# Causal masks of the first tiles and the first six head pairs as a VectorE product, and the first sequence loaded by head pair with weight quarters between

## The chip, the cores and the metric

The kernel runs on one core of one Trainium2 chip. The metric is device time in microseconds (us) of one execution, the median of several. A profiled span (314.4 us for the kernel before) is a little shorter than the timed execution (315.6 us), so spans are compared with spans and times with times.

Engine names in the profile: PE is TensorE (matmuls), PEld is TensorE loading weights, DVE is VectorE, ACT is ScalarE, POOL is GpSimd, SP is SyncE.

## The reference

Two stages. Attention with chunk selection: each query takes the 6 chunks of 32 keys (out of 24) with the highest upper bound, under a causal mask. Then a feed-forward layer with a squared ReLU over all tokens.

```python
batch, n_heads, seq, head_dim = 4, 8, 768, 64          # attention
n_tokens, d_model, d_ff = 3072, 512, 2048              # feed-forward

ub = sum(max(q * k_min[chunk], q * k_max[chunk]))      # upper bound of each chunk
ub = where(query_chunk >= chunk, ub, -1e9)
top_chunks = argsort(ub)[-6:]
mask = selected(top_chunks) & (query >= key)
attn = softmax(where(mask, q @ k.T / 8, -1e9))
x = attn @ v                                           # heads side by side: (3072, 512)
out = relu(x @ w_in) ** 2 @ w_out
```

## The kernel before

Inputs are fp32 in HBM and bf16 on chip. Loads that convert are issued by GpSimd, one instruction for each load. A sequence has 768 tokens, that is 6 tiles of 128, and 8 heads, handled as 4 head pairs; 4 sequences make 16 pairs.

The first tile of every sequence needs no selection, because it has only four chunks; the kernel does these tiles first, and their feed-forward runs beside the attention of sequence 0. From then on the attention of one sequence runs beside the feed-forward of the one before it. The feed-forward of the last sequence runs alone at the end.

The loads: first tiles of k, q, v for two sequences at a time, then the other tiles of sequence 0 as one load for each tile of all heads, then weights, then the other sequences.

```python
def load_rest(nm, b, j):            # one tile of 128 tokens, all 8 heads: 128 KB as bf16
    ...
    nc.gpsimd.dma_start(
        out=nat[nm, b][:, j - 1, :, 0:D],
        in_=SRC[nm][b, :, 128 * j:128 * (j + 1)].rearrange("h p d -> p h d"))
# ... (first loads and constants cut)
for nm in "kq":
    for j in range(1, NT):
        load_rest(nm, 0, j)
load_w_in(4, 8)
```

The causal mask of a diagonal 128x128 block is a GpSimd instruction, in the same stream as the load issues. It stands between the exponential (ScalarE) and the product with v (TensorE):

```python
def causal(e, n):
    nc.gpsimd.affine_select(
        out=e, in_=e, compare_op=ALU.is_ge, fill=0.0, base=0,
        channel_multiplier=-1, pattern=[[0, n], [1, 128]])
# first tiles, for each sequence b and half hh of the pairs:
    nc.scalar.activation(e, ps, ACT.Exp, scale=scale)
    causal(e, NP)                                     # 128x512
# pairs, for each of five banks of scores, four of which hold diagonal blocks:
    nc.scalar.activation(e, ps, ACT.Exp, scale=scale)
    if diagonal:
        causal(e[:, 128*d0:128*d1]..., d1 - d0)       # 128x128 or 128x256
    run_ffn()                                         # some feed-forward units
    behind.append(lambda: values(...))                # product with v, three banks later
    if i % 2 == 0:
        beside()                                      # next piece of the next pair's selection
```

The selection of a pair (stage a) transposes k on TensorE, takes chunk maxima and minima on VectorE (`kr`, 0.95 us each), transposes q, forms its positive and negative parts (`qp`, `qm`), multiplies for the upper bounds (`ub`), takes the top 8 of each row and turns the selection into extra rows of q, from which the scores (`ps`) then follow. The order of instructions on each engine is fixed when the kernel is built, by a scheduler. In the traces below each engine takes its instructions in that order, so one that waits holds those behind it: in the run loads_only, eight masks that stand behind loads in GpSimd's stream begin only at 40.05 us, when the last of those loads has been issued.

The softmax here doesn't subtract the row's maximum and nothing guards it: scores larger than these inputs give would overflow.

## Time and profile before

| | before |
|---|---|
| time, median | 315.6 us |
| first scores of pair 0 | 35.91 us |
| first 320-column up-projection: end of the first sequence's stage | 98.5 us |
| the same for the next two sequences | 158.6, 217.2 us |
| span of the profile | 314.4 us |

The first-tile feed-forward uses 512-column matmuls, the later ones 320-column matmuls, so the first 320-column up-projection marks the moment when the first sequence is done and the next begins. The steady stage takes 58.6 us. Lines of TensorE's timeline, from three stretches (start us, duration us, what): the last q transpose of pair 0, its first scores, and the first 320-column up-projection.

```profile
28.34 0.29 PE L246 MATMUL qT<-ident,qn 128*128 128x128 bf16 x1 [0.55 <-DMA qn<-in_q_dram]
35.91 1.04 PE L398 MATMUL ps<-qsc,kqc 88*128 88x256 bf16 x4
98.53 0.71 PE L315 MATMUL ph<-xT,w_in_sb 128*128 128x320 bf16 x4
```

The page of the kernel before, part 2: busy tenths in 40 slices of 7.86 us, and the mean DMA share.

```profile
PE   0554887898888999999999999999999999899995
POOL 8966962999968011111120111212011122000000
DMA  9999999999999100010100000111000011100021
GB/s 68 174 168 125 134 189 196 155 131 137 171 148 109 11 1 2 2 67 35 68 3 3 0 2 33 41 62 36 2 0 2 2 68 36 67 0 2 14 89 67
```

GpSimd is at 9 in slices 8 to 11 (55 to 86 us), and TensorE doesn't reach 9 for good until slice 14 (102 us). The engines' busy times in stretches of the start and the first sequence, and of a steady stretch at the end (after the stretch and its length, one column each for PE, PEld, DVE, ACT and POOL: busy us and, in brackets, instructions; then granted clock, DMA share, GB/s):

```profile
24.00:36.00 12.00, 6.95 (x66) 4.74 (x67) 10.06 (x38) 2.34 (x4) 9.67 (x16) 1.00 1.20 109
46.00:56.00 10.00, 7.44 (x68) 4.00 (x66) 7.60 (x24) 6.88 (x13) 3.87 (x10) 1.00 1.55 194
56.00:66.00 10.00, 9.47 (x86) 5.84 (x89) 6.30 (x25) 7.57 (x14) 10.00 (x18) 0.83 2.41 154
66.00:76.00 10.00, 8.73 (x87) 5.26 (x87) 6.05 (x13) 6.39 (x12) 10.00 (x17) 1.00 1.92 123
160.00:200.00 40.00, 38.68 (x374) 25.47 (x374) 29.63 (x103) 30.73 (x64) 6.25 (x20) 1.00 0.04 14
```

From 56 to 76 us GpSimd never rests. The chain of waits of the kernel before in that stretch, in order of time (start us, duration us, what), shows what it does:

```profile
...
61.47 1.59 POOL e L168 x5
63.06 0.86 POOL vn L86
63.92 0.89 POOL kn L86
64.81 0.55 POOL e L168 x2
65.36 0.84 POOL kn L86
66.20 0.67 POOL e L168
66.87 2.61 POOL kn L86 x3
...
```

Masks (`e L168`) stand between load issues (`L86`) of the next sequences' tiles at about 0.9 us each. Who pays is in the list of waits of the weight loads between 36 and 99 us (total us, times, longest us):

```profile
PEld L381 <- POOL e L168: 7.9, 7, 3.1
```

The product with v takes a masked tile as its weights; it waits seven times, 7.9 us in all, and the matmuls of that product wait with it.

### The profile page before, as it was taken

How to read it: one execution, taken by the hardware profiler on the slowest of the kernel's cores; microseconds unless marked ns; L12 is line 12 of the kernel's file. 1: busy time of each engine (PE TensorE's matmuls, PEld its weight loads, DVE VectorE, ACT ScalarE, POOL GpSimd, SP SyncE). 2: the span in 40 equal slices, each digit the busy share in tenths (PEclk: the TensorE clock that was granted, in tenths of full speed). 3: DMA queues.
4: the chain of work that ended last, by engine and by line, in shares of the span. 5: the costliest groups of instructions: out<-in, count | busy, mean ns of one | idle time of the engine just before them, and what ended most of it. 6: DMA issues, size and time to landing. Idle time of an engine off the chain costs nothing.

```text
span 314.4 us, 6653 instructions
## 1 busy us (share of the span) xinstructions
PE 276.2 (88%) x2503; PEld 171.8 (55%) x2528; DVE 183.6 (58%) x595; ACT 189.4 (60%) x370; POOL 112.0 (36%) x222
## 2 busy tenths in 40 slices
PE   0554887898888999999999999999999999899995
PEld 0332644555446666655677665557676555566542
DVE  0117978485647888646598886657887640455200
ACT  2212267586466879666597886567789666377311
POOL 8966962999968011111120111212011122000000
PEclk9999999799999999999999999999999999999999
DMA  9999999999999100010100000111000011100021
GB/s 68 174 168 125 134 189 196 155 131 137 171 148 109 11 1 2 2 67 35 68 3 3 0 2 33 41 62 36 2 0 2 2 68 36 67 0 2 14 89 67
DMA packets 82188, 20.61 MB, mean 66 GB/s; under 512 B 75332, under 2 KB 78572, under 8 KB 82156
## 3 DMA queue, kind: packets, MB, share of 16 engines
q0 software_dynamic: 78448, 13.64, 55.2%
q1 hardware_dynamic: 3708, 6.55, 5.7%
q8 instruction: 20, 0.33, 0.4%
q14 instruction: 12, 0.10, 0.1%
HBM read 27.26 MB, written 6.29 MB: 107 GB/s over the span
## 4 chain that ended last, share of the span: by engine, by line
PE 48%; POOL 17%; DMA 11%; DVE 11%; ACT 8%; issue 3%; ACTq 0%; POOLq 0%
PE ph L315 18%; PE py L330 16%; DMA w_out_sb<-in_moe_w_out_dram 6%; POOL vn L86 5%; PE ps L398 5%; DVE kr L234 5%; ACT qsc L254 4%; PE av L381 4%; POOL qn L86 4%; DMA w_in_sb<-in_moe_w_in_dram 4%; POOL e L168 3%; DVE kqc L231 3%; POOL kn L86 3%; ACT ht L320 2%; DMA qn<-in_q_dram 2%
## 5 line engine op out<-in xcount | busy, mean ns | idle before, releaser
L405 ACT ACTIVATE e<-ps 128x512 bf16<-128x512 f32 x160 | 92.4, 601 | 51.9 <-PE ps L398 50.3
L315 PE MATMUL ph<-xT,w_in_sb 128*128 128x320 bf16 (+1 forms) x572 | 98.6, 307 | 1.2 <-issue 0.2
L168 POOL TENSOR_SCALAR_AFFINE_SELECT e<-e 128x128 bf16<-128x128 bf16 (+2 forms) x136 | 47.3, 356 | 143.1 <-ACT e L405 140.5
L330 PE MATMUL py<-w_out_sb,h 128*128 128x512 bf16 x363 | 94.0, 378 | 0.9
L320 ACT ACTIVATE ht<-ph 128x320 bf16<-128x320 f32 (+1 forms) x144 | 64.7, 457 | 25.2 <-PE ph L315 16.1
L315 PEld LDWEIGHTS <-w_in_sb 128*128 128x128 bf16 x576 | 55.3, 97 | 29.1 <-issue 7.3
L398 PE MATMUL ps<-qsc,kqc 88*128 88x128 bf16 (+1 forms) x320 | 61.8, 278 | 0.5
L323 DVE TENSOR_TENSOR h<-ht 128x320 bf16<-128x320 bf16 (+1 forms) x144 | 47.2, 339 | 22.7 <-ACT ht L320 21.6
L381 PEld LDWEIGHTS <-e 128*128 128x128 bf16 x640 | 38.3, 98 | 30.8 <-POOL e L168 9.6
L330 PEld LDWEIGHTS <-h 128*128 128x128 bf16 x384 | 36.5, 97 | 29.0 <-issue 0.2
L381 PE MATMUL av<-vn,e 128*128 128x65 bf16 x480 | 38.6, 194 | 6.7 <-POOL e L168 6.3
L234 DVE TENSOR_REDUCE kr<-kT 128x24 bf16<-128x768 bf16 x32 | 29.2, 951 | 0.2
L231 DVE COPY kqc<-kT 64x768 bf16<-64x768 bf16 x32 | 17.7, 553 | 15.9 <-PE kT L227 15.4
L335 ACT COPY ob<-py 128x512 f32<-128x512 f32 x24 | 14.0, 585 | 21.1 <-PE py L330 21.0
L398 PEld LDWEIGHTS <-kqc 88*128 88x128 bf16 x320 | 23.1, 100 | 4.1 <-issue 1.8
L254 ACT COPY qsc<-qT 64x640 bf16<-64x640 bf16 x32 | 21.8, 681 | 0.2
L175 DVE RECIPROCAL rc<-av 128x5 f32<-128x5 f32 (+1 forms) x40 | 7.5, 188 | 23.4 <-PE av L381 23.2
L86 POOL DMA_DIRECT2D qn<-in_q_dram x20 | 18.0, 908 | 8.1 <-DMA w_out_sb<-in_moe_w_out_dram 5.0
L265 DVE TENSOR_TENSOR ubm<-ub,ubmask 128x240 f32<-128x240 f32 x16 | 6.5, 405 | 22.6 <-PE ub L262 22.3
L176 DVE TENSOR_TENSOR x<-av,rc 128x320 bf16<-128x320 f32 (+1 forms) x40 | 18.9, 472 | 0.7
L86 POOL DMA_DIRECT2D kn<-in_k_dram x20 | 18.1, 918 | 2.7 <-DMA w_in_sb<-in_moe_w_in_dram 2.7
L282 DVE COPY qsc<-sT 24x640 bf16<-24x640 bf16 x32 | 15.5, 484 | 4.5 <-PE sT L278 3.5
(54 smaller groups left out, 214.7 us busy)
## 6 DMA issues: line engine op xcount, KB each, us to landing
out_dram<-ob SPq DMA_DIRECT2D x24, 256.0 KB, 2.6
kn<-in_k_dram POOLq DMA_DIRECT2D x20, 128.0 KB, 7.3
qn<-in_q_dram POOLq DMA_DIRECT2D x20, 128.0 KB, 5.4
vn<-in_v_dram POOLq DMA_DIRECT2D x20, 128.0 KB, 5.0
w_out_sb<-in_moe_w_out_dram POOLq DMA_DIRECT2D x2, 1024.0 KB, 15.7
w_in_sb<-in_moe_w_in_dram POOLq DMA_DIRECT2D x2, 512.0 KB, 9.5
w_in_sb<-in_moe_w_in_dram POOLq DMA_DIRECT2D x1, 1024.0 KB, 9.3
k<-in_k_dram POOLq DMA_DIRECT2D x2, 256.0 KB, 6.6
```

What stands on the lines that cost most here:

```text
L86: nc.gpsimd.dma_start(out=nat[nm, b][:, j - 1, :, 0:D], in_=SRC[nm][b, :, 128 * j:128 * (j + 1)].rearrange("h p d -> p h d"))
L168: nc.gpsimd.affine_select(out=e, in_=e, compare_op=ALU.is_ge, fill=0.0, base=0, channel_multiplier=-1, pattern=[[0, n], [1, 128]])
L231: nc.vector.tensor_copy(kqs[0:D, s, hh], pt[D * hh:D * hh + D])
L234: nc.vector.tensor_reduce(kr[:, mm], pt.rearrange("d (c j) -> d c j", j=CH), axis=AX.X, op=op)
L254: nc.scalar.copy(qss[0:D, s, hh], pt[D * hh:D * hh + D])
L315: nc.tensor.matmul(ph, lhsT=w_in_sb[:, ki, 128 * f:128 * (f + 1)], rhs=xT[:, ki, c0:c1], start=(ki == 0), stop=(ki == NKI - 1))
L320: nc.scalar.activation(ht, ph, ACT.Relu)
L323: nc.vector.tensor_mul(h2[f][:, c0:c1], ht, ht)
L330: nc.tensor.matmul(py, lhsT=h2[f][:, 128 * t:128 * (t + 1)], rhs=w_out_sb[:, f, :], start=(f == 0), stop=(f == NFI - 1))
L381: nc.tensor.matmul(av[:, t - 1], lhsT=e[:, 128 * c:128 * (c + 1)], rhs=value_tile(b, 2 * hp + hh, j), start=(i == 0 and c == 0), stop=(i = ...
L398: nc.tensor.matmul(ps[:, 128 * c:128 * (c + nt)], lhsT=kqs[:, s, hh, 128 * j:128 * (j + 1)], rhs=qss[:, s, hh, 128 * (t0 - 1):128 * (t0 - ...
L405: nc.scalar.activation(e, ps, ACT.Exp, scale=scale)
```

## The change

Its intent: take the masks out of the GpSimd stream until GpSimd has issued all loads (pair 6), and load sequence 0 in the order in which it is used, one head pair at a time, with a quarter of a weight matrix between pairs. Loads of sequence 1 then go out in one run. Six copies of k go from VectorE to ScalarE to make room on VectorE for the masks.

```diff
+    def load_pair(nm, b, hp):                       # 2 loads of 80 KB as bf16
+        for h in (2 * hp, 2 * hp + 1):
+            nc.gpsimd.dma_start(
+                out=rest(nm, b)[:, :, h, 0:D],
+                in_=SRC[nm][b, h, 128:].rearrange("(j p) d -> p j d", p=128))
 ...
     load_first("q", 0, 2)
-    load_first("v", 0, 2)
     load_first("k", 2, 4)
     load_first("q", 2, 4)
+    load_first("v", 0, 2)
     load_first("v", 2, 4)
     load_w_in(0, 4)
+    tri = consts.tile([128, 128], BF16, tag="tri")   # 1 on and above the diagonal
 ...
-    for nm in "kq":
-        for j in range(1, NT):
-            load_rest(nm, 0, j)
-    load_w_in(4, 8)
-
-    def causal(e, n):
-        nc.gpsimd.affine_select(...)
+    for hp in range(NP):
+        load_pair("k", 0, hp)
+        load_pair("q", 0, hp)
+        if hp < 3:
+            load_w_in(4 * hp + 4, 4 * hp + 8)
+        else:
+            load_w_out(0, 4)
+        load_pair("v", 0, hp)
+    for f in range(4, NFI, 4):
+        load_w_out(f, f + 4)
+
+    def causal(e, n, early):
+        if early:
+            nc.vector.tensor_mul(
+                e, e, tri.unsqueeze(1).to_broadcast([128, n, 128]))
+        else:
+            nc.gpsimd.affine_select(...)
 ...
-            causal(e, NP)
+            causal(e, NP, True)                       # first tiles
 ...
-            nc.vector.tensor_copy(kqs[0:D, s, hh], pt[D * hh:D * hh + D])
+            if p < 3:
+                nc.scalar.copy(kqs[0:D, s, hh], pt[D * hh:D * hh + D])
+            else:
+                nc.vector.tensor_copy(kqs[0:D, s, hh], pt[D * hh:D * hh + D])
 ...
-                        "p (n j) -> p n j", j=128), d1 - d0)
+                        "p (n j) -> p n j", j=128), d1 - d0, p < 6)
 ...  # v of sequence 0 and the weights are no longer among the loads issued pair by pair
-    loads(6)
+    loads(15)
 ...
-        loads(8)
+        loads(5)
```

More of the change, by code (lines that the diff above doesn't have):

```diff
@@ L76, in load_first, with rest @@
             in_=SRC[nm][b0:b1, :, 0:128].rearrange("b h p d -> p (b h) d"))
-    def load_rest(nm, b, j):
+    def rest(nm, b):
         if (nm, b) not in nat:
@@ L85, in load_rest, with load_tile @@
                         "p j h o -> p (j h) o"), 1.0)
+        return nat[nm, b]
+    def load_tile(nm, b, j):
         nc.gpsimd.dma_start(
-            out=nat[nm, b][:, j - 1, :, 0:D],
+            out=rest(nm, b)[:, j - 1, :, 0:D],
             in_=SRC[nm][b, :, 128 * j:128 * (j + 1)].rearrange("h p d -> p h d"))
+    def load_pair(nm, b, hp):
[3 more added lines that the diff above has]
+                in_=SRC[nm][b, h, 128:].rearrange("(j p) d -> p j d", p=128))
     def key_tile(nm, b, hp, j):
@@ L115 @@
     load_first("q", 0, 2)
-    load_first("v", 0, 2)
     load_first("k", 2, 4)
     load_first("q", 2, 4)
+    load_first("v", 0, 2)
     load_first("v", 2, 4)
     load_w_in(0, 4)
+    tri = consts.tile([128, 128], BF16, tag="tri")
+    nc.gpsimd.memset(tri, 1.0)
+    nc.gpsimd.affine_select(
+        out=tri, in_=tri, compare_op=ALU.is_ge, fill=0.0, base=0,
+        channel_multiplier=-1, pattern=[[1, 128]])
     kqs = consts.tile([KC, NSET, 2, S], BF16, tag="kqs", name="kqc")
@@ L159 @@
         )
-    for nm in "kq":
-        for j in range(1, NT):
-            load_rest(nm, 0, j)
-    load_w_in(4, 8)
-    def causal(e, n):
-        nc.gpsimd.affine_select(
-            out=e, in_=e, compare_op=ALU.is_ge, fill=0.0, base=0,
-            channel_multiplier=-1, pattern=[[0, n], [1, 128]])
+    for hp in range(NP):
[13 more added lines that the diff above has]
+        else:
+            nc.gpsimd.affine_select(
+                out=e, in_=e, compare_op=ALU.is_ge, fill=0.0, base=0,
+                channel_multiplier=-1, pattern=[[0, n], [1, 128]])
     def normalise(av, n, x):
@@ L433 @@
     later = []
-    for j in range(1, NT):
-        later.append(lambda j=j: load_rest("v", 0, j))
-        if j == 2:
-            later.append(lambda: load_w_in(8, NFI))
-    later.append(lambda: load_w_out(0, 8))
-    later.append(lambda: load_w_out(8, NFI))
     for b in range(1, B):
@@ L442 @@
             for j in range(1, NT):
-                later.append(lambda nm=nm, b=b, j=j: load_rest(nm, b, j))
+                later.append(lambda nm=nm, b=b, j=j: load_tile(nm, b, j))
     def loads(n):
```

## The prediction

> **What bounds it now.** From 160 to 250 us (stage view) TensorE is 97% busy, and a sequence takes 58.6 us (first up-projection runs of two sequences on the chain of waits: 161.4, 220.1). The last 40 us are feed-forward alone. Neither changes. The loss is before 102 us, where the first sequence ends.
>
> 1. *Start, 0 to 36 us.* The first selected scores come at 35.9 us (timeline). They need head pair 0 only, but its q comes as tiles of all heads: the last q transpose waits for a tile landing at 28.3 us (tiles land 0.83 us apart). Then 7.3 us of transposes, top-k and copies.
> 2. *First sequence, 36 to 102 us, 66 us.* It has 33 feed-forward units against 41.25; a unit is four 512-column matmuls, 0.215 us from start to start (0.86 us), so at the steady pace it takes 58.6 - 7.1 = 51.5 us. The chain from 54.9 to 90 us is nearly all GpSimd: DMA issues of 0.91 us with the masks queued between them. Weight loads of masked tiles wait 9.1 us for GpSimd, up to 3.1 us at once.
>
> **What the change does.**
> - Takes 56 masks off GpSimd: 8 of 128x512 (0.63 us), 48 in the pairs (0.31 to 0.43 us). On VectorE the squares took 327 ns for 320 columns and 435 for 512, 0.56 ns a column; I estimate 0.22, 0.29 and 0.44 us for 128, 256 and 512 columns, 15 us in all. The Trainium skill ("VectorE: DVE Perf Modes", the perf-mode tier table) caps a bf16 tensor_tensor at two elements a cycle; the slope agrees. VectorE is 64% busy in steady stages and has room. Six 64x768 copies go to ScalarE (about 0.75 us each).
> - Pair 0's k and q: six first loads (about 1.9 us each), a weight quarter (2.5), four 80 KB loads (0.5 each at the tile rate): near 22 us, not 28.3.
> - First-tile masks no longer wait for GpSimd until 23.7 us; but VectorE has masks, normalising, reduces, x copies and top-k nearly without a gap from 16.5 us. I put the first scores at 30 to 31 us.
> - Bytes are the same. A pair with its quarter needs about 5.6 us of DMA and as much GpSimd issue (0.8 us each): first sequence and weights are in by 50 us, w_out before its use near 58. Later loads hold no mask.
>
> **On the critical path.** Start: 5 us. First sequence: 66 to about 53 us (steady pace plus some waits), 13 us. Second: 59.4 us now, at most 0.7. Sum 17 to 18 us: 298 us, 292 to 305 in 8 of 10. Chances: faster 0.94, same 0.05, slower 0.01.
>
> **What would show it.** Right: first selected scores near 30 us; first 320-column up-projection near 84 us; mask waits under 3 us in the first sequence; TensorE over 90% busy from 35 us; later sequences 58.6 us. Wrong, by step: scores at 34 or later; a first sequence over 58 us with waits for VectorE masks, stuck in its in-order stream behind 0.95 us reduces and unfinished exponentials; small loads landing over 0.8 us apart; waits for w_out near 58 us.
>
> **What would make it wrong.** More GpSimd issue time per small load than 0.8 us, so that DMA starves; VectorE's queue replacing GpSimd's; the Trainium skill ("SBUF — State Buffer", the "DVE blocks DMA" trap) says that GpSimd cannot write descriptors while VectorE runs in a two-port mode, which no view of this trace isolates; a throttled clock (0.79 at 56 to 64 us) returning for longer.

## The result, and the profile after

| | before | after | predicted |
|---|---|---|---|
| time, median | 315.6 us | 302.7 us | 298 (292 to 305) |
| first scores of pair 0 | 35.91 us | 32.57 us | 30 to 31 |
| first 320-column up-projection | 98.5 us | 86.1 us | 84 |
| the same for the next two sequences | 158.6, 217.2 us | 145.7, 204.3 us | 58.6 apart |
| span of the profile | 314.4 us | 301.5 us | |

The ratio of after to before is 0.959 (95% interval 0.957 to 0.962). Ratios here are the mean time of one kernel's fast runs over that of the other's of the same rounds, so not quite the ratio of the medians that are quoted.

The gain of the span, 12.9 us, can be read off the rows: 3.3 us before the first scores, 9.1 us in the first sequence (62.6 us before, 53.5 after), 0.5 us in the second (60.1 to 59.6), nothing later (58.6 both times).

The same parts of the page for the kernel after (slices of 7.54 us), its first 320-column up-projection, and the same stretches:

```profile
PE   0574999999999999999999999999999999899995
POOL 8969993999850001111301112212012122000000
```

```profile
86.08 0.70 PE L342 MATMUL ph<-xT,w_in_sb 128*128 128x320 bf16 x4
```

```profile
24.00:36.00 12.00, 7.45 (x52) 4.93 (x54) 8.08 (x30) 4.70 (x8) 11.51 (x15) 1.00 1.83 170
46.00:56.00 10.00, 9.45 (x91) 5.54 (x92) 8.58 (x33) 9.93 (x19) 5.95 (x8) 1.00 1.92 176
56.00:66.00 10.00, 9.52 (x97) 5.82 (x98) 8.01 (x23) 7.12 (x14) 9.94 (x13) 1.00 2.43 155
66.00:76.00 10.00, 9.71 (x95) 5.86 (x94) 8.66 (x32) 5.83 (x11) 9.51 (x12) 1.00 2.24 185
```

TensorE is at 9 from slice 5 on (30 us). GpSimd is nearly as busy from 56 to 76 us as it was, with load issues and a few memsets, and no mask; but TensorE is now at 9.5 and 9.7 of 10 us there. The loads still take nearly all of GpSimd's time; but hardly anything on the path of the matmuls waits behind them. The list of waits of the weight loads between 33 and 86 us of the kernel after has a single entry for masked tiles, now from VectorE:

```profile
PEld L408 <- DVE e L189: 0.5, 1, 0.5
```

0.5 us instead of 7.9. The start is another matter. These are the first scores of pair 0 (L425), in the timeline of TensorE of the kernel after, and the VectorE timeline before them:

```profile
22.34 0.62 PE L273 MATMUL qT<-ident,qn 128*128 128x128 bf16 x4
32.57 1.06 PE L425 MATMUL ps<-qsc,kqc 88*128 88x256 bf16 x4
```

```profile
23.75 0.93 DVE L261 TENSOR_REDUCE kr<-kT 128x24 bf16<-128x768 bf16 x1
24.59 0.41 DVE L200 TENSOR_TENSOR x<-av,rc 128x256 bf16<-128x256 f32 x1
25.01 0.93 DVE L261 TENSOR_REDUCE kr<-kT 128x24 bf16<-128x768 bf16 x1
25.85 0.41 DVE L200 TENSOR_TENSOR x<-av,rc 128x256 bf16<-128x256 f32 x1
26.18 0.25 DVE L264 TENSOR_TENSOR kbd<-kr,own 128x96 bf16<-128x96 bf16 x1
26.35 0.48 DVE L278 TENSOR_SCALAR qp<-qT 128x640 bf16<-128x640 bf16 x1
```

The last q transposes of pair 0 began at 22.34 us, six us earlier than before, so the loads did their part. But `qp`, which needs nothing else, began at 26.35 us. VectorE was busy with the reduces of k and the normalising of the first tiles (`x`).

### The profile page after: what moved, and what is told of

Same layout as the page of the kernel before. It is cut to its first block, busy times and chain, and to the rows that moved or that the text cites. A ratio compares the mean times of both kernels' runs of the same rounds, so it can differ in the third digit from the quotient of the medians.

```text
span 301.5 us, 6654 instructions
## 1 busy us (share of the span) xinstructions
PE 272.0 (90%) x2503; PEld 171.4 (57%) x2528; DVE 189.2 (63%) x645; ACT 192.9 (64%) x376; POOL 102.0 (34%) x180
## 4 chain that ended last, share of the span: by engine, by line
PE 54%; DVE 20%; ACT 14%; issue 4%; POOL 4%; DMA 3%; ACTq 0%; POOLq 0%
PE ph L342 19%; PE py L357 18%; DVE kr L261 7%; PE ps L425 6%; ACT qsc L281 5%; ACT e L432 5%; PE av L408 4%; DVE kqc L258 4%; ACT ht L347 3%; DVE h L350 3%; DMA qn<-in_q_dram 3%; PE xt L334 2%; PE sT L305 2%; PE qT L273 2%; DVE m L296 1%
## 5 line engine op out<-in xcount | busy, mean ns | idle before, releaser
L192 POOL TENSOR_SCALAR_AFFINE_SELECT e<-e 128x128 bf16<-128x128 bf16 x80 | 25.9, 323 | 142.3 <-ACT e L432 142.3
L425 PE MATMUL ps<-qsc,kqc 88*128 88x128 bf16 (+1 forms) x320 | 60.9, 274 | 0.7 <-ACT e L432 0.4
L350 DVE TENSOR_TENSOR h<-ht 128x320 bf16<-128x320 bf16 (+1 forms) x144 | 46.0, 333 | 18.7 <-ACT ht L347 17.5
L357 PEld LDWEIGHTS <-h 128*128 128x128 bf16 x384 | 36.5, 97 | 28.9 <-issue 0.2
L425 PEld LDWEIGHTS <-kqc 88*128 88x128 bf16 x320 | 23.0, 99 | 3.8 <-issue 1.5
L258 DVE COPY kqc<-kT 64x768 bf16<-64x768 bf16 x26 | 14.4, 553 | 6.8 <-PE kT L251 6.4
L309 DVE COPY qsc<-sT 24x640 bf16<-24x640 bf16 x32 | 15.5, 484 | 4.9 <-PE sT L305 4.1
L189 DVE TENSOR_TENSOR e<-e,tri 128x128 bf16<-128x128 bf16 (+2 forms) x56 | 13.8, 259 | 3.5 <-ACT e L432 3.3
L408 PE MATMUL av<-v,e 128*128 128x65 bf16 x160 | 15.7, 194 | 0.0
```

Of the source, the lines that this page charges most:

```text
L192: nc.gpsimd.affine_select(out=e, in_=e, compare_op=ALU.is_ge, fill=0.0, base=0, channel_multiplier=-1, pattern=[[0, n], [1, 128]])
L258: nc.vector.tensor_copy(kqs[0:D, s, hh], pt[D * hh:D * hh + D])
L350: nc.vector.tensor_mul(h2[f][:, c0:c1], ht, ht)
L357: nc.tensor.matmul(py, lhsT=h2[f][:, 128 * t:128 * (t + 1)], rhs=w_out_sb[:, f, :], start=(f == 0), stop=(f == NFI - 1))
L408: nc.tensor.matmul(av[:, t - 1], lhsT=e[:, 128 * c:128 * (c + 1)], rhs=value_tile(b, 2 * hp + hh, j), start=(i == 0 and c == 0), stop=(i = ...
L425: nc.tensor.matmul(ps[:, 128 * c:128 * (c + nt)], lhsT=kqs[:, s, hh, 128 * j:128 * (j + 1)], rhs=qss[:, s, hh, 128 * (t0 - 1):128 * (t0 - ...
```

## The experiments

My theory after the result: two gains that add, an earlier start from the loads and a shorter first sequence from the masks. The rivals: the masks do it all, or the loads do it all. A second question came up on the way: what sets the end of the first sequence once the masks wait no more. Twelve kernels ran; all gave correct results.

| kernel | time (us) | ratio to before, 95% interval | first scores | first 320-column | first sequence |
|---|---|---|---|---|---|
| after | 302.7 | 0.957 to 0.962 | 32.6 | 86.1 | 53.5 |
| masks_only | 305.3 | 0.964 to 0.968 | 34.5 | 87.3 | 52.8 |
| loads_only | 324.0 | 1.023 to 1.027 | 28.7 | 106.4 | 77.8 |
| first_masks_back | 318.1 | 1.004 to 1.009 | 28.6 | 99.9 | 71.3 |
| pair_masks_back | 314.0 | 0.991 to 0.996 | 32.1 | 98.4 | 66.3 |
| copies_back | 303.2 | 0.957 to 0.962 | 33.4 | 86.0 | 52.7 |
| quarters_behind | 304.8 | 0.962 to 0.968 | 32.1 | 89.1 | 57.0 |
| xt_act | 303.7 | 0.957 to 0.963 | 33.7 | 86.7 | 53.0 |
| topk_first | 302.9 | 0.955 to 0.961 | 29.4 | 85.9 | 56.4 |
| pe_first | 310.7 | 0.980 to 0.984 | 40.3 | 93.2 | 52.9 |
| pe_two | 309.9 | 0.977 to 0.981 | 40.2 | 92.3 | 52.2 |
| masks_all | 304.3 | 0.960 to 0.963 | 32.1 | 85.5 | 53.4 |
| pe_grouped_two | 299.9 | 0.946 to 0.954 | 30.3 | 82.4 | 52.1 |

The last column is the difference of the two before it. The last three columns are read from one profiled execution each; times and ratios are of all executions. The runs were made on different chips, each with the kernel before beside it, so the ratios are the fairer comparison. For loads_only and first_masks_back the last column misleads: their first scores come early, but the exponential of these scores begins only at 46.3 and 45.6 us.

### masks_only: the masks without the loads

The kernel before, with this:

```diff
+    tri = consts.tile([128, 128], BF16, tag="tri")   # built as in the kernel after
-            causal(e, NP)
+            causal(e, NP, True)
-                        "p (n j) -> p n j", j=128), d1 - d0)
+                        "p (n j) -> p n j", j=128), d1 - d0, p < 6)
```

> The kernel before with the masks of the first tiles and of pairs 0 to 5 on VectorE; loads, their order and the copies as before. Theory 1 (two gains that add: an earlier start from loading by pair, a shorter first sequence from freeing GpSimd's queue): first selected scores still at 35 to 36 us, since q of pair 0 lands at 28.3 us as before; first sequence (first scores to first 320-column up-projection) 53 to 56 us instead of 62.6; total 306 to 309 us. Rival, the masks do it all: 302 to 304 us. Rival, the loads do it all: 313 to 316 us.

It took 305.3 us, 3.4% under the kernel before, against 4.1% for the whole change. First scores came at 34.5 us and the first sequence took 52.8 us. So the masks alone are most of the gain, and shorten the first sequence by as much as the whole change does. The total lies between the ranges of the theory and of the rival "masks do it all", a little below the theory's. The first scores came 1.4 us earlier than in the kernel before with the loads as they were, which the theory had not expected: part of the gain at the start is the masks' too.

### loads_only: the loads without the masks

The kernel after, with all masks on GpSimd and the copies on VectorE:

```diff
-            causal(e, NP, True)
+            causal(e, NP, False)
-                        "p (n j) -> p n j", j=128), d1 - d0, p < 6)
+                        "p (n j) -> p n j", j=128), d1 - d0, False)
-            if p < 3:
+            if False:
```

> The kernel after with all masks on GpSimd and the six copies back on VectorE, so that only the loads differ from before. The build puts the eight first-tile masks behind 31 loads in GpSimd's stream. Theory 1: these masks come near 42 us, the first sequence starts late or stalls, and the pair masks queue behind tile loads again; total 314 to 322 us: loading by pair is worth nothing while masks share the queue. Rival, the loads do it all: 302 to 306 us.

It took 324.0 us: the loads alone lose 2.5%, more than I expected. The first scores came early, at 28.7 us, but the GpSimd timeline of this kernel shows where the eight first-tile masks stand (the L192 line):

```profile
36.04 1.71 POOL L95 DMA_DIRECT2D vn<-in_v_dram  x2 [0.20 <-issue]
37.74 2.26 POOL L117 DMA_DIRECT2D w_out_sb<-in_moe_w_out_dram  x3
40.05 4.74 POOL L192 TENSOR_SCALAR_AFFINE_SELECT e<-e 128x512 bf16<-128x512 bf16 x8
44.75 4.41 POOL L89 DMA_DIRECT2D kn<-in_k_dram  x5
```

They begin at 40 us, behind the last weight quarter (a place that this build gave them; another place between the loads was not tried), and everything that follows from the first tiles waits for them: the first up-projection came at 54.2 us, against 30.0 in the kernel after. With copies_back below as the fourth corner (masks and loads, copies on VectorE as in these two), the four corners are 1, 0.966 (masks), 1.025 (loads) and 0.960 (both): loading by pair loses 2.5% with masks on GpSimd and gains 0.7% without them (0.9595 over 0.9661).

### first_masks_back and pair_masks_back: one half of the masks back on GpSimd

The kernel after, with `causal(e, NP, False)` for the first tiles, or with `False` in place of `p < 6` for the pairs.

> The kernel after with only the eight first-tile masks back on GpSimd; they stand behind 31 loads in its stream. Theory 1: first values wait for masks at about 42 us instead of 17 us; first scores of pair 0 by 33 us if TensorE's stream lets them pass, else near 45 us; total 306 to 314 us. Rival (first-tile masks do not matter, pair masks do): 302 to 304 us.

> The kernel after with only the masks of pairs 0 to 5 back on GpSimd, behind 25 tile loads of the next two sequences. Theory 1: first scores at 32.6 us as in the kernel after, then mask waits of over 10 us in pair 0, which reaches its masks only when GpSimd has issued those loads (near 70 us); total 312 to 325 us. Rival (pair masks do not matter): 302 to 305 us.

With the first-tile masks back: 318.1 us, worse than expected and slower than the kernel before. With the pair masks back: 314.0 us, in the expected range. (The profiled execution had a clock of 0.962; but the other three, at 0.988 to 0.993, took 313.3 to 315.1 us, so the clock isn't what makes it slow.) In the second, GpSimd's first pair mask begins at 64.0 us, and the list of waits of the weight loads from 32 to 98 us has the mask waits again, larger than before (11.8 us in 15 waits, the longest 5.7 us; over 10 us in pair 0 alone had been expected):

```profile
PEld L408 <- POOL e L192: 11.8, 15, 5.7
```

So in this order of the stream, with the masks behind the loads, neither half can stay there. The loads in their new order depend on both halves having left.

### copies_back: the six copies back on VectorE

```diff
-            if p < 3:
+            if False:
```

> The kernel after with the six 64x768 copies of pairs 0 to 2 back on VectorE. The kernel with masks alone has its first scores at 34.5 us though its q lands 6 us later than in the kernel after (32.6 us), so the start of the kernel after is held by VectorE's own work, not by the loads. Theory (start bound by VectorE): two copies more in that chain put the first scores at 33.5 to 34 us; total 303.5 to 305 us. Rival (ScalarE, 90 to 99% busy from 32 to 56 us, bounds pairs 0 and 1, and the copies hurt it): first scores at most 1 us later, first sequence 1 to 2 us shorter than 53.5 us; total 301 to 302.5 us.

It took 303.2 us with a ratio of 0.960, the same as the kernel after within the interval. First scores came 0.8 us later, and the first sequence was 0.8 us shorter. Neither theory's total was met: moving the copies to ScalarE helps the start and costs the same afterwards. No gain of the six copies shows in the total.

### quarters_behind: the weights after the pairs

```diff
     for hp in range(NP):
         load_pair("k", 0, hp)
         load_pair("q", 0, hp)
-        if hp < 3:
-            load_w_in(4 * hp + 4, 4 * hp + 8)
-        else:
-            load_w_out(0, 4)
         load_pair("v", 0, hp)
     for f in range(4, NFI, 4):
+        load_w_in(f, f + 4)
+    for f in range(0, NFI, 4):
         load_w_out(f, f + 4)
```

> The kernel after with the weight quarters after all four pairs of the first sequence, instead of between them. Theory (weights are needed at their unit, and 80 KB loads alone leave the DMA engines short because GpSimd issues one each 0.88 us): the second w_in quarter lands near 44 us instead of 25 us, the fifth up-projection unit, due near 37 us, waits about 7 us for it; DMA moves near 100 to 130 GB/s while the pairs are loaded; total 307 to 312 us. Rival (the order is slack): 302 to 303.5 us.

It took 304.8 us, 0.6% more than the kernel after by the ratios (0.965 to 0.959), with intervals that just touch. The TensorE timeline shows the wait, in brackets, 2.3 us instead of the 7 expected:

```profile
41.18 1.47 PE L340 MATMUL ph<-xT,w_in_sb 128*128 128x512 bf16 x4 [2.30 <-DMA w_in_sb<-in_moe_w_in_dram]
```

From 12 to 42 us DMA moved 141 GB/s here and 174 GB/s in the kernel after. The total lies between the ranges of the theory and of the rival. (The profiled execution took 306.2 us, 1.4 us above the median, so its first sequence of 57.0 us is a little long.) The direction was right, the size of the wait a third: the second w_in quarter was there by 41 us, not 44, and TensorE came to the unit that needs it at 38.9 us, not 37.

### xt_act: four copies at the start on ScalarE

```diff
-            nc.vector.tensor_copy(xT[:, :, 128 * t:128 * (t + 1)], pt)
+            (nc.scalar.copy if n == B else nc.vector.tensor_copy)(
+                xT[:, :, 128 * t:128 * (t + 1)], pt)
```

> The kernel after with the four 128x512 copies of the transposed first-tile rows on ScalarE, idle at that time. Theory (start bound by VectorE): 1.6 us less in its chain before the first scores; first scores at 31 to 31.5 us; total 301 to 301.8 us. Rival (start bound by loads or by GpSimd): first scores unchanged at 32.6 us; total 302.3 to 303 us.

It took 303.7 us, no gain, and the first scores came later, at 33.7 us. The copies did leave VectorE, and the first up-projection came at 27.5 us instead of 30.0. But the scheduler then put the squares of these early units ahead of the selection of pair 0 in VectorE's order, and VectorE waited for them (`h`, L351), between the top 8 (L296) and the last copy before the scores (L309):

```profile
29.03 0.95 DVE L296 MAX8 m<-ubm 128x8 f32<-128x24 f32 x10
30.43 0.43 DVE L351 TENSOR_TENSOR h<-ht 128x512 bf16<-128x512 bf16 x1 [0.45 <-ACT ht L348]
30.77 0.40 DVE L297 TENSOR_TENSOR selb<-ubm,m 128x240 bf16<-128x240 f32 x1
32.13 0.43 DVE L351 TENSOR_TENSOR h<-ht 128x512 bf16<-128x512 bf16 x1 [0.96 <-ACT ht L348]
33.21 1.00 DVE L309 COPY qsc<-sT 24x640 bf16<-24x640 bf16 x2 [0.65 <-PE sT L305]
```

So this run doesn't test what it was made for.

### topk_first: the selection of pair 0 earlier in VectorE's order

```diff
     first_scores(3)
+    aside.append((0, stage_a(0)))
+    finish_a(0)
     first_values(2)
     first_values(3)
 ...
     loads(15)
-    aside.append((0, stage_a(0)))
```

> The kernel after with the selection of pair 0 written before the values of the last two first-tile batches, so that VectorE does qp, the reduces and the top-k of pair 0 ahead of half of the normalising and of all four x copies. The work is the same. Theory (start bound by the order of VectorE's stream): qp begins by 24 us instead of 26.4, first scores at 29 to 30.5 us; feed-forward starts about as late as now; total 299.5 to 301.5 us. Rival (loads or GpSimd bound the start): 302.3 to 303 us.

The first scores came at 29.4 us, as the theory of VectorE's order had it: that order did hold the start. And the total was 302.9 us, as the rival had it. The feed-forward of the first tiles began later instead (33.7 us against 30.0), and at the end of the first sequence, 85.9 us, nothing was left of the 3.1 us. An earlier first score isn't by itself an earlier end. The likely reason, argued and not tested alone, is that the first sequence has two kinds of work, and here what the scores gained, the feed-forward lost (3.7 us). pe_grouped_two below has both kinds earlier.

### pe_first and pe_two: masks added by TensorE

The mask can also be a matrix of -32768 above the diagonal, added to the scores in PSUM by a product with the identity, before the exponential.

```diff
                 nc.tensor.matmul(ps[:, hp], lhsT=t[rows, 0, hp],
-                                 rhs=t[rows, 1, hp], start=True, stop=True)
+                                 rhs=t[rows, 1, hp], start=True, stop=False)
+                nc.tensor.matmul(ps[:, hp], lhsT=ident, rhs=negtri,
+                                 start=False, stop=True)
 ...
-            causal(e, NP, True)
```

pe_two does the same for the diagonal blocks of pairs 0 and 1, after the scores of a bank, and puts the six copies back on VectorE.

> The kernel after with the eight first-tile masks neither on GpSimd nor on VectorE: a 128x128 tile of -32768 above the diagonal is added to the scores by one more TensorE product per head, before the exponential. It takes 2.9 us of VectorE work away ahead of the first scores (8 masks of 0.36 us, start to start) and a wait of ScalarE, VectorE, TensorE in a row, at 32 small matmuls where TensorE is idle. Theory (pairs 0 and 1 are held by VectorE and ScalarE together, so less work for them is a gain, while the earlier experiments that only moved work or its order gave none): first up-projection at 27 us instead of 30, first scores near 30 us; total 300 to 301.5 us. Rival (something after pair 1, the same in all variants, sets the end of the first sequence at 86 us): 302.3 to 303 us.

> As pe_first, and the masks of pairs 0 and 1 added by TensorE too (10 products of 128 columns a pair, 0.54 us of TensorE), with the six copies back on VectorE, so that both VectorE and ScalarE have less to do in pairs 0 and 1 (ScalarE 3.2 us less, VectorE about the same). Theory: pairs 0 and 1 take 12 us each instead of 12.5, total 299 to 301 us. Rival (TensorE is the bound there, and pays 1.1 us more): no better than pe_first, or 0.5 to 1 us worse.

Both lost to the kernel after, 7 to 8 us by the medians and 6 to 7 by the ratios, where a gain was expected. The first scores of pair 0 came at 40 us. The TensorE timeline of pe_first shows why:

```profile
11.35 0.28 PE L231 MATMUL ps<-t 64*128 64x128 bf16 x1
11.56 0.29 PE L233 MATMUL ps<-negtri,ident 128*128 128x128 bf16 x1
11.79 0.29 PE L231 MATMUL ps<-t 64*128 64x128 bf16 x1
12.01 0.29 PE L233 MATMUL ps<-negtri,ident 128*128 128x128 bf16 x1
...
```

Scores over 64 rows and masks over 128 rows alternate, 0.22 us from start to start. In the kernel after eight score matmuls in a row take 0.62 us in three of the four batches, and 1.02 us in the fourth:

```profile
11.61 0.62 PE L226 MATMUL ps<-t 64*128 64x128 bf16 x8
```

The eight are two runs of four, one for each half of the 128 rows. In the trace their starts come in twos, 0.013 us apart (11.607 and 11.620, 11.686 and 11.700 us), and within each half the step is 0.107 us, the same as between two transposes over 128 rows at this time. So 0.22 is to be set against 0.107 us: alternation doubles the step, and the scores also lose their running in twos.

The Trainium skill ("TensorEngine Tiling (Array Packing)", Available Configurations and Key Properties) says that changing the tiling mode drains TensorE, and lists 64-row and 128-row modes. That agrees with what is seen here. Runs of transposes with a new weight tile for each matmul keep the step of 0.107 us (four in 0.6 us in the kernel after), so it isn't the new weights alone. Nor is it only that a mask is added to scores just written: the step from a mask to the next scores, which write other columns, is as long (0.23 us, 11.56 to 11.79).

Pairs 0 and 1 of pe_two took 11.0 and 11.5 us, against 12.5 and 12.4 in the kernel after (first exponential to first exponential); pair 2 took 12.8 against 11.6. All three together are 1.2 us shorter. But copies_back, which only moved the copies as pe_two does, is already 0.8 us shorter there (35.7 against 36.5 us), which leaves 0.4 us to the masks.

### masks_all: all masks on VectorE

```diff
-                        "p (n j) -> p n j", j=128), d1 - d0, p < 6)
+                        "p (n j) -> p n j", j=128), d1 - d0, True)
```

> The kernel after with the masks of all 16 pairs on VectorE, none on GpSimd, which then only loads. VectorE gets 80 more masks, 18 us in 170 us, in stages where it is 64 to 78% busy. Theory (steady stages are held by TensorE, VectorE has room): within 1 us of the kernel after, 302 to 303.7 us. Rival (VectorE in its fixed order delays the masks and so TensorE): 304 to 308 us.

304.3 us, ratio 0.961, with an interval (0.960 to 0.963) that overlaps that of the kernel after (0.957 to 0.962). The median is in the rival's range, the ratio (0.7 us more than the kernel after) in the theory's, so the totals don't decide. The stages do: the first 320-column up-projections of the next two sequences are at 145.0 and 204.5 us, so a steady sequence takes 59.5 us, not 58.6. So the 80 masks on VectorE aren't free: they cost 0.9 us in each steady sequence. And nothing is gained, since GpSimd is free there anyway.

### pe_grouped_two: runs of one kind, and less work for VectorE

As pe_two, with the scores of both halves first and then one wide mask product for each half; the copies of pair 0 stay on ScalarE (`p < 1`).

```diff
         for hh in range(2):
             ...
             for hp in range(NP):                                # eight scores in a row
                 nc.tensor.matmul(pss_[hh][:, hp], lhsT=t[rows, 0, hp],
                                  rhs=t[rows, 1, hp], start=True, stop=True)
+        for hh in range(2):
+            nc.tensor.matmul(
+                pss_[hh], lhsT=ident,
+                rhs=negtri.unsqueeze(1).to_broadcast([128, NP, 128]),
+                start=False, stop=True, skip_group_check=True)
 ...  # pairs 0 and 1, after the scores of a bank
+                by_pe = diagonal and p < 2
+                if by_pe:
+                    for d in range(*diagonal):
+                        nc.tensor.matmul(
+                            ps[:, 128 * d:128 * (d + 1)], lhsT=ident,
+                            rhs=negtri, start=False, stop=True,
+                            skip_group_check=True)
```

> pe_first lost 8 us because its first-tile products over 64 rows (scores) and over 128 rows (mask) alternate, 0.22 us from start to start against 0.06 us for runs of one kind. Here the scores of both halves come first, eight products, then the mask as one 512-column product for each half; the masks of pairs 0 and 1 go to TensorE too, after their scores, and the copies of pairs 1 and 2 are back on VectorE (pair 0's stay on ScalarE, idle then). Theory (alternation was the loss; less VectorE and ScalarE work ahead of and in pairs 0 and 1 is a gain): the eight first-tile score groups take 1.5 to 2.5 us a batch instead of 3.3; first scores near 30 us, first 320-column up-projection at 82 to 84 us (86.1 in the kernel after, 92.3 in pe_two); total 298.5 to 301 us, under both kernels. Rival (something else made pe_first slow, or the end of the first sequence near 86 us is fixed by another cause): 302 us or more.

It took 299.9 us (299.1 to 302.6 over six runs), ratio 0.950 (0.946 to 0.954), below both kernels; the interval doesn't overlap that of the kernel after. In the TensorE timeline eight scores take 0.62 us again and two masks of 512 columns about 1 us:

```profile
11.20 0.62 PE L231 MATMUL ps<-t 64*128 64x128 bf16 x8
11.74 1.04 PE L234 MATMUL ps<-negtri,ident 128*128 128x512 bf16 x2
```

The first scores came at 30.3 us. That is later than in topk_first (29.4), and yet the first sequence ended 3.5 us earlier (82.4 against 85.9). Pairs 0 to 2 took 11.0, 11.7 and 12.3 us, 35.1 in all, against 36.5 in the kernel after. So of the gain of 3.7 us over the kernel after, 2.3 us are an earlier start of pair 0 (first exponential at 30.9 against 33.2 us) and 1.4 us shorter pairs. Here the feed-forward also began earlier (first up-projection at 26.0 us against 30.0), unlike in topk_first, and the earlier start lasted.

topk_first changed only the order of the work and gained nothing; here 24 masks have left VectorE and two pairs' copies have left ScalarE. copies_back shows that moving the copies alone leaves the end where it was. What this run doesn't separate is how much came from the first-tile masks and how much from the pair masks. A further difference is TensorE's own pace. Early in every run 128-column matmuls in a row are 0.107 us apart, later about 0.055 (in the kernel after with a granted clock of 1.00 at both times); that change comes at 15.9 us here, with a relapse from 26.0 to 28.1, and at 34.2 us in the kernel after. I estimate what the slow pace cost from the first up-projection on, as half of the slow step for the columns of each slow matmul: 1.3 us here and 1.9 us in the kernel after. From there on it explains some 0.6 of the 3.7 us; what it did before that was not measured.

## Why the prediction was right, and where it was off

The time, 302.7 us, lies in the range, 4.7 us above the centre. The mechanism for the masks held; that the total is in the range is also owed to a range wide enough for two mis-sized terms, both too large. Point by point:

- *Mask waits.* Right. Predicted under 3 us in the first sequence, 0.5 us found. The mechanism, masks queued between load issues on GpSimd, is shown by masks_only and by both runs that put masks back (the latter also place them behind more loads).
- *Cost of a mask on VectorE.* Right. Estimated at 0.22, 0.29 and 0.44 us, found at 0.22, 0.28 and 0.42 us. From 128 to 512 columns that is 0.52 ns a column, which agrees with two elements a cycle in the Trainium skill ("VectorE: DVE Perf Modes", the perf-mode tier table) at the 0.96 GHz that it gives for VectorE ("Trainium Kernel Development and Optimization", NeuronCore Architecture): an estimate of 0.52 ns from these two figures.
- *TensorE over 90% busy from 35 us.* Right: 9.35 to 9.71 of every 10 us from 36 to 86 us.
- *First sequence, "66 to about 53 us", 13 us.* The 53 was right: 53.5 us. The 66 was a misreading. I took 102.06 us as the end of the first sequence from the longest pieces of the chain of waits; the first 320-column up-projection is a shorter piece, at 98.5 us. The stage took 62.6 us before, and the gain was 9.1 us. This is the larger part of the miss.
- *Start, "5 us".* Mis-sized: 3.3 us. The data came when predicted (last q transposes at 22.3 us), but I put VectorE's stream at 30 to 31 us and it needed until 32.6, between the mark for right (near 30) and the mark for wrong (34 or later). topk_first shows that its order held the first scores, and also that an earlier first score bought with a later feed-forward is worth nothing in the end: 3.1 us gained there left the total where it was.
- *What the two parts of the change are worth.* The prediction gave the start to the loads and the sequence to the masks, as if they added. masks_only has 83% of the gain by its ratio (3.4 of 4.1%); loads_only is a loss. The first scores of masks_only, at 34.5 us, put 1.4 of the 3.3 us of the start down to the masks as well. The loads are worth 0.7% on top of the masks (copies_back against masks_only), and minus 2.5% without them.
- *Issue time of small loads.* Estimated at 0.8 us, found at 0.89 (L95 groups, 128x5x64). No starvation followed with the quarters between. Without them DMA fell to 141 GB/s.
- *Later sequences 58.6 us, second at most 0.7 us.* Right: 58.6 and 0.5 us.
- *SBUF port.* The Trainium skill ("SBUF — State Buffer", the "DVE blocks DMA" trap) made me list a risk. No run here isolates it; tile load issues took 0.91 to 0.92 us before and 0.90 to 0.93 us after, in the stretch from 55 to 90 us, so it didn't show.

What stays open is what exactly sets the end of the first sequence at 86 us in the kernel after. The traces narrow it down: from the first exponential of pair 3 to the first 320-column up-projection it takes 16.3 us in the kernel after, masks_only, copies_back, topk_first, masks_all, quarters_behind, pe_first, pe_two and pe_grouped_two alike, against 17.8 in the kernel before. So what these runs differ in lies before pair 3. Reordering (topk_first) and moving work between VectorE and ScalarE (copies_back) left it at 85.9 to 86.1, removing work from both moved it to 82.4. From 46 to 56 us ScalarE is busy 9.93 of 10 us and TensorE 9.45. That fits a stage which several engines fill together, but no run took work from one engine alone without giving it to another.

## What to carry to other kernels

An engine that issues loads and also does a small step on the path of the matmuls makes each step wait for the issues queued ahead of it; move the step before reordering the loads, since here the better load order alone, with the masks left behind the loads, cost 2.5%. Mark the stages of a pipeline by an instruction that starts them, not by the longest piece in a view, and measure a start gain at the end of the stage that follows: 3 us of earlier first scores were worth nothing where the feed-forward began 3.7 us later, and 2.3 us lasted where it began earlier too. When a step is moved to TensorE, keep matmuls of the same row count in runs.

## What the Trainium skill lacked or had wrong

- "TensorEngine Tiling (Array Packing)" says that a change of tiling mode drains TensorE, without a size. Here 128-column matmuls over 64 and 128 rows in alternation took 0.22 us each from start to start, against 0.107 us in runs of one kind at the same time of the run. For the 64 matmuls of pe_first that is an estimate of 7 us, close to what this kernel lost (7 to 8 us).
- "DMA: Bandwidth & Descriptors" gives, in its breakdown of the fixed cost of a GpSimd-issued load, about 50 ns for the sequencer's dispatch and calls descriptor generation small and variable; the breakdown is of latency and doesn't say how long GpSimd is held. Here the issue held GpSimd 0.79 to 0.86 us for a load of 512 rows of 2 KB, 0.89 us for 640 rows of 256 B, 0.91 us for 1024 and 1.2 us for 2048 rows of 256 B, and GpSimd instructions behind it waited. No page was found that warns of a compute step on GpSimd behind a run of loads.
- The two pages used for VectorE's rate agreed with the runs; the trap on the SBUF page was not tested by any.
